# A retention block and a channel mix in one written order: mu's loads on SyncE, block 2 in another form, all pieces in a new order

## The chip, the cores and the metric

The kernel runs on one core of a Trainium2 chip. The metric is the device time of one execution in microseconds (us); lower is better. The core has TensorE (PE, matrix products, with its weight loads shown apart as PEld), VectorE (DVE), ScalarE (ACT), GpSimd (POOL) and SyncE (SP). Here POOL and SP do no arithmetic: they issue transfers (DMAs) between the chip's memory (HBM) and the core's memory (SBUF). PE writes its results to PSUM, eight banks of 512 float32 a partition.

## The reference

Inputs q, k, v have shape (4, 8, 768, 64): batch, heads, time, width. The first stage carries a 64 x 64 state per head through time, and its output, with the heads side by side (512 wide), is the input x of the second stage.

```python
for t in range(S):
    state = gamma[None, :, None, None] * state + np.einsum('bhd,bhe->bhde', k[:, :, t], v[:, :, t])
    y[:, :, t] = scale * np.einsum('bhd,bhde->bhe', q[:, :, t], state)
...
xk = mu_k * x + (1.0 - mu_k) * x_prev
xr = mu_r * x + (1.0 - mu_r) * x_prev
k = np.maximum(xk @ w_k, 0.0)
v = k * k @ w_v
r = 1.0 / (1.0 + np.exp(-(xr @ w_r)))
return (r * v).astype(np.float32)
```

x_prev is x one time step earlier; w_k is 512 x 1024, w_v 1024 x 512, w_r 512 x 512. The output is 4 x 768 x 512 float32.

## The kernel before

Time is cut into blocks of 256 tokens: three to a batch, twelve in all, n = 0 to 11. The step-by-step recurrence is replaced by products within a block (scores of q and k under a causal mask, then times v) and by a state carried between the three blocks of a batch. Blocks 0, 3, 6, 9 begin a batch and need no state; blocks 2, 5, 8, 11 end one and pass none on.

Nothing is scheduled by a compiler. The string ORDER (lines 28 to 79) lists all pieces of work, and the loop at lines 809 to 824 emits them one by one. Each engine executes its own pieces in that order, and waits at a piece whose inputs aren't there, so that what stands behind it on the same engine waits too. A word is code.arguments, with `@` and digits for the PSUM banks and `~` and a letter for the engine (v DVE, a ACT, p POOL, s SP). The first argument is the block n. The codes:

- `lq`, `lk`, `lv` (line 239) load q, k, v of a block. Those on POOL convert q and k to float16 on the way. The first half of block 0's q and k (heads 0 to 3, `lq.0.0.2` and `lk.0.0.2`) comes over SP as float32 into a staging place, and `cq`, `ck` (line 266) convert it on ACT. `mu` (line 739) loads mu_k and mu_r in four small transfers, issued by ACT in before.
- `Tq`, `Tk` (line 294) transpose on PE; `Eq`, `Ek` (lines 320 to 340) copy the result to SBUF on ACT. `tq`, `tk` transpose by DMA, issued by SP, for blocks 9 to 11.
- `vs` (line 276) scales v, on DVE. `S` are the scores (line 378, PE), `M` masks them (line 412, DVE).
- `C` is the block's contribution to the state (line 436, PE), `U` sums it (line 469, mostly DVE), `G` decays it (line 484).
- `I`, `Y`, `J` are the block's output on PE: from the state (`I`, `J`) and from the masked scores times v (`Y`). `I.2` reads the result of `U.2.0`. `D` (line 564, DVE) brings it to SBUF as x, transposed.
- `dx` and `X.n.w.j` (lines 588 and 607, DVE) form xk (w = 0) and xr (w = 1), a quarter j of the width each.
- `K.n.g` (line 627, PE) is a piece of xk @ w_k and needs all four X.n.0.*; `Qa`, `Qb` (ACT) take relu and square. `R` (PE) and `s` (ACT) are the gate, and need X.n.1.*. `V` (PE) is the product with w_v, `O` (DVE) multiplies with the gate, `st` stores over SP. `Vc`, `Oc`, `sc` do the last half block in two column halves.
- `wk`, `wr`, `wv` load the weights over POOL, wk in two halves. `gy` are powers of gamma.
- `z.c` (line 755) multiplies zeros into a bank that nobody reads: c // 4 float32 products and c % 4 float16 ones, 512 columns each, a float32 one counting as four units. They use no data and fill time on PE.

A block has one of three forms, by two lists at lines 17 and 22. Blocks 6 to 11 (HALF) treat a block as four chunks of 64 tokens. Blocks in WIDE (2 to 5 in before) are held with one half of the tokens on the partitions per load: each of k and v comes in two transfers, whose rows are 256 bytes (one token of one head), and the scores are 16 products of 128 weight columns. The remaining ones (0 and 1) hold two neighbouring tokens per partition: one transfer with rows of 512 bytes, and 32 score products of 64 weight columns. Which form a block takes is asked for in `split` (line 235), `scale_v`, `scores`, `masked`, `state` and `intra` (lines 276 to 560).

Of the kernel before, what the change touches and what calls it, by code (L numbers as in the profile page):

```python
# [39 lines left out]
R.1.0@2 R.1.1@3 Qb.1.1 s.1.0 Tq.3@2 s.1.1 Eq.3~a C.3@67 Tk.3@4 Ek.3~a R.0.0@3 s.0.0 Tk.4@2  # L40
S.3.0@01 wv.0~p dx.2~v X.2.0.0 X.2.0.2 X.2.0.1 X.2.0.3 X.2.1.1 S.3.1@45 Ek.4~a K.2.0@3 lq.7~p
Tq.4@2 M.3.1~v U.3.0~a U.3.1 Qa.2.0 wv.1~p Eq.4~a K.2.3@6 Qa.2.3 M.3.0~v K.2.1@7 S.4.1@45
S.4.0@23 vs.4~v M.4.0~v K.2.2@6 Qb.0.2 I.3@01 Y.3 C.4@23 G.3~a M.4.1~v U.4.0 lk.5~p Qb.1.0
Qa.2.2 V.1.0.0@6 lq.5~p I.4@45 Qa.2.1 Qb.2.1 X.2.1.3 J.3 D.3~v Y.4 V.0.1.0@7 V.0.0.0@0 J.4 U.4.1
Tq.7@23 Eq.7~a V.1.1.0@1 V.1.1.1 G.4~a Qb.2.0 dx.3~v V.0.0.1 Tk.5@2 Ek.5~a D.4~v dx.4~v V.0.1.1
Qb.2.3 V.1.0.1 Tq.5@2 X.3.0.3 X.3.0.1 X.3.0.2 Eq.5~a X.3.0.0 K.3.1@3 Qa.3.1 K.3.3@4 O.1.1 O.0.0
S.5.0@01 O.1.0 O.0.1 lv.5~p lq.6~p M.5.0~v S.5.1@23 vs.5~v K.3.2@5 Qa.3.3 lk.6~p Qb.3.3 K.3.5@4
M.5.1~v X.2.1.0 Qa.3.2 X.2.1.2 Tq.6@67 Qa.3.5 Tk.6@01 Eq.6~a lv.6~p lv.7~p Ek.6~a C.5@5 U.5.0
X.3.1.0 Qb.3.1 K.3.0@4 Qa.3.0 lk.7~p K.3.7@6 S.6@23 Qb.3.2 M.6~v I.5@01 Y.5 vs.6~v V.2.1.0@7
R.2.1@2 lv.10~p Qb.2.2 Qa.3.7 K.3.4@6 st.0.0 vs.7~v Qb.3.7 s.2.1 st.0.1 V.2.1.1 Tk.7@45 Qb.3.5  # L50
Qa.3.4 X.3.1.3 X.3.1.1 Qb.3.0 C.6@23 st.1.0 J.5 Ek.7~a X.3.1.2 R.2.0@6 lv.8~p U.6.0~a D.5~v
U.6.1 U.6.2 U.6.3 V.2.0.0@4 s.2.0 K.3.6@6 dx.5~v Qa.3.6 lq.8~p lk.8~p st.1.1 R.4.1@5 I.6@01
O.2.1 st.2.1 X.5.0.1 s.4.1 G.6~a V.2.0.1 O.2.0 X.5.1.0 X.5.0.3 R.3.1@6 s.3.1 C.7@23 U.7.0 S.7@45
Y.6 M.7~v V.3.1.0@7 X.5.0.2 D.6~v R.4.0@6 lk.9~p Qb.3.4 vs.8~v V.3.0.0@4 R.3.0@5 X.5.1.2 s.4.0
Qb.3.6 V.4.1.0@6 V.3.0.1 V.3.1.1 X.5.1.3 V.4.1.1 U.7.1 U.7.2 X.5.1.1 I.7@01 U.7.3 Tk.8@23 O.3.1
s.3.0 O.3.0 R.5.1@7 Ek.8~a st.3.1 lv.9~p dx.6~v X.5.0.0 s.5.1 C.8@45 Tq.8@23 Y.7 K.5.0@7 O.4.1
vs.9~v st.4.1 Eq.8~a D.7~v K.5.3@6 dx.7~v X.6.0.2 G.7~v Qa.5.0 Qb.5.0 st.2.0 lq.10~p tq.10~s
K.5.1@7 Qa.5.1 X.6.0.3 X.6.0.1 Qa.5.3 K.5.2@2 Qa.5.2 st.3.0 lk.10~p tk.10~s lv.11~p U.8.0 U.8.1
U.8.2 R.5.0@7 tk.9~s s.5.0 X.6.0.0 V.4.0.0@6 V.4.0.1 O.4.0 Qb.5.1 lk.11~p lq.9~p Qb.5.3
V.5.0.0@7 V.5.1.0@2 S.8@01 M.8~v I.8@45 X.6.1.3 Qb.5.2 V.5.0.1 K.6.4@6 X.6.1.1 O.5.0 Qa.6.4  # L60
K.6.7@3 Qa.6.7 K.6.3@6 Qa.6.3 X.6.1.0 lq.11~p X.6.1.2 K.6.1@3 Qa.6.1 Y.8 D.8~v C.9@01 Qb.6.1
vs.10~v U.9.0~a S.10@67 M.10~v U.9.1 dx.8~v X.8.0.3 X.8.0.2 Qb.6.3 K.6.6@3 X.8.0.0 Qb.6.7 Qa.6.6
Qb.6.6 V.5.1.1 K.6.2@4 Qa.6.2 X.8.0.1 Qb.6.2 K.6.5@3 tq.9~s Qa.6.5 R.6.1@4 s.6.1 tq.11~s st.5.0
K.6.0@6 O.5.1 U.9.2 U.9.3 G.9~v R.6.0@7 s.6.0 R.7.1@4 Qb.6.4 s.7.1 st.5.1 K.8.3@7 Qa.8.3 S.9@23
tk.11~s I.9@45 Qa.6.0 Qb.6.0 Qb.6.5 C.10@01 U.10.0 M.9~v R.7.0@7 s.7.0 U.10.1 U.10.2 U.10.3
K.8.2@6 K.8.1@2 Qa.8.1 vs.11~v Qb.8.1 V.6.0.0@7 Y.9 I.10@01 C.11@23 G.10~v V.6.0.1 Qa.8.2
V.7.1.0@6 D.9~v K.8.0@4 Qa.8.0 Qb.8.0 Qb.8.2 U.11.0 U.11.1 U.11.2 V.7.1.1 dx.9~v O.7.1 st.7.1
Qb.8.3 I.11@23 Y.10 D.10~v dx.10~v X.9.0.0 S.11@45 M.11~v X.9.0.2 V.7.0.0@6 V.7.0.1 V.6.1.0@0
V.6.1.1 V.8.0.0@1 V.8.0.1 X.9.0.1 V.8.1.0@4 V.8.1.1 st.4.0 X.9.0.3 K.9.0@5 O.7.0 K.9.4@6 X.9.1.1
Qa.9.0 Qa.9.4 Qb.9.4 X.9.1.0 O.6.0 st.6.0 Qb.9.0 X.9.1.3 X.8.1.2 Y.11 X.9.1.2 O.6.1 K.9.2@5  # L70
Qa.9.2 Qb.9.2 K.9.6@6 Qa.9.6 X.8.1.3 K.9.7@7 Qa.9.7 Qb.9.7 K.9.1@0 Qa.9.1 Qb.9.1 K.9.3@5 Qa.9.3
Qb.9.3 R.10.0@7 R.9.1@0 s.9.1 st.6.1 D.11~v R.9.0@5 s.9.0 st.7.0 X.8.1.1 K.9.5@6 V.10.1.0@5
Qa.9.5 Qb.9.5 Qb.9.6 V.10.0.0@6 X.8.1.0 dx.11~v R.8.1@0 s.8.1 V.9.1.0@2 R.8.0@0 X.11.0.2
X.11.1.3 X.11.0.0 X.11.0.3 X.11.0.1 K.11.1@3 s.8.0 K.11.3@0 Qa.11.3 O.8.0 st.8.0 s.10.0
V.9.0.0@1 Qa.11.1 Qb.11.1 K.11.2@0 Qa.11.2 O.8.1 st.8.1 K.11.0@7 X.11.1.2 V.10.0.1 Qb.11.2
# [7 lines left out]
def kernel(  # L83
# [543 lines left out]
    def keys(e, n, g, u=None):  # L627
# [11 lines left out]
        for i in range(w):  # L639
            fo = w * g + i  # L640
            for co in range(NCO):
# [3 lines left out]
                    start=(i == 0 and co == 0), stop=(co == NCO - 1), skip_group_check=True,  # L645
                )

    def relued(e, n, g, *u):
# [2 lines left out]
        nc.scalar.activation(out=kr, in_=banks("K", n, g, *u), func=AF.Relu)  # L651
# [87 lines left out]
    def load_mu(e):  # L739
        for w, x in enumerate((moe_mu_k, moe_mu_r)):  # L740
            y = x.rearrange("(x r c) -> x r c", x=2, c=D)
            for hp in range(2):
                nc.scalar.dma_start(
                    out=mu8[w * NCO : (w + 1) * NCO, low(hp)], in_=y[:, 1:3] if hp else y[:, 0:4:3]
                )

# [108 lines left out]
```

## Time and profile before

| | us |
|---|---|
| median of 3 runs (155.16 to 155.71) | 155.42 |
| the profiled execution | 155.54 |
| its span, first to last instruction | 153.7 |
| PE busy | 147.1 |
| DVE busy | 128.1 |
| ACT busy | 94.4 |
| POOL busy | 62.1 |

A row of the timeline gives start, length, engine, line, operation, output<-input and, in brackets, how long the engine had been idle and what released it. A name with a q behind the engine (SPq, ACTq, POOLq) is a transfer's issue. The chain of work that ended last is followed back from the last instruction; each of its pieces has a start and a length. The engine's busy time counts products of zeros like any other.

### The profile page before, as it was taken

What the parts mean: (1) busy time and instruction counts of PE and PEld (TensorE: products, weight loads), DVE (VectorE), ACT (ScalarE), POOL (GpSimd) and SP (SyncE); (2) the same over time, 40 slices, a digit from 0 to 9 for tenths busy, and PEclk for the clock granted to TensorE, in tenths of its full rate; (3) what the DMA queues carried; (4) which work ended last, traced back from release to release, by engine and by line L of the source; (5) the groups of instructions that cost most, each with busy time, mean ns of one, the idle gap of its engine ahead of it and who ended that gap; (6) DMA issues with size and microseconds to landing.
All of it is one profiled execution on the core that took longest, in us unless ns stands there. A gap on an engine that the chain in (4) does not pass through costs nothing.

```text
span 153.7 us, 4956 instructions
## 1 busy us (share of the span) xinstructions
PE 147.1 (96%) x2129; PEld 82.7 (54%) x2129; DVE 128.1 (83%) x204; ACT 94.4 (61%) x172; POOL 62.1 (40%) x77
## 2 busy tenths in 40 slices
PE   7799899999999999999999999999999999999991
...
DVE  1379999999989999999999996999999999421551
...
GB/s 138 264 234 194 182 237 235 157 196 203 194 188 203 249 226 194 11 236 156 255 178 249 219 156 161 183 62 106 35 4 141 0 70 141 0 0 136 68 205 136
DMA packets 56525, 23.83 MB, mean 155 GB/s; under 512 B 48056, under 2 KB 52024, under 8 KB 56504
## 3 DMA queue, kind: packets, MB, share of 16 engines
...
q10 hardware_dynamic: 456, 0.32, 0.8%
...
HBM read 24.31 MB, written 6.29 MB: 199 GB/s over the span
## 4 chain that ended last, share of the span: by engine, by line
PE 70%; DVE 14%; DMA 6%; ACT 4%; issue 2%; ACTq 2%; DVEq 0%
PE ps L684 24%; PE ps L672 12%; PE ps L632 10%; PE ps L642 9%; DMA kT<-k 6%; DVE a L417 3%; DVE xk L618 3%; DVE dx L592 2%; DVE vs L277 2%; PE ps L504 2%; PE ps L765 2%; DVE xT L577 2%; PE ps L308 2%; PE ps L372 1%; PE ps L303 1%
## 5 line engine op out<-in xcount | busy, mean ns | idle before, releaser
L684 PE MATMUL ps<-wv,k2s 128*128 128x512 f16 x184 | 43.9, 380 | 0.2 <-ACT kr L651 0.2
L651 ACT ACTIVATE kr<-ps 128x512 f32<-128x512 f32 x48 | 27.8, 594 | 23.4 <-PE ps L632 14.9
L684 PEld LDWEIGHTS <-k2s 128*128 128x128 f16 x184 | 17.3, 98 | 19.1
L690 DVE SCALAR_TENSOR_TENSOR os<-ps,rs 128x512 f32<-128x512 f32 x23 | 15.1, 683 | 12.9 <-PE ps L684 6.5
L672 PE MATMUL ps<-wr,xr 128*128 128x512 f16 x96 | 24.0, 380 | 0.0
L642 PE MATMUL ps<-xk,wk 128*128 128x256 f16 x192 | 23.6, 273 | 0.1
L256 POOL DMA_DIRECT2D v<-in_v_dram x20 | 18.0, 917 | 13.8 <-DVE vs L277 10.9
L632 PE MATMUL ps<-xk,wk 128*128 128x512 f16 x96 | 22.8, 380 | 0.0
L417 DVE TENSOR_TENSOR a<-ps,c_sb 128x1024 f16<-128x1024 f32 (+1 forms) x20 | 21.8, 1109 | 0.8 <-PE ps L393 0.8
L678 ACT ACTIVATE rs<-ps 128x512 f32<-128x512 f32 x24 | 14.3, 594 | 11.4 <-PE ps L672 8.8
L642 PEld LDWEIGHTS <-wk 128*128 128x128 f16 x192 | 18.1, 98 | 4.4 <-DVE xk L618 0.5
L618 DVE SCALAR_TENSOR_TENSOR xr<-dx,mu,xT 128x256 f16<-128x256 f32 (+1 forms) x36 | 19.3, 564 | 0.0
L618 DVE SCALAR_TENSOR_TENSOR xk<-dx,mu,xT 128x256 f16<-128x256 f32 (+1 forms) x36 | 18.9, 567 | 0.3
L256 POOL DMA_DIRECT2D k<-in_k_dram x20 | 17.8, 916 | 2.6 <-DMA wv<-in_moe_w_v_dram 1.2
L277 DVE TENSOR_TENSOR vs<-v,csm_sb 128x1024 f16<-128x1024 f32 x12 | 14.5, 1214 | 2.7 <-DMA v<-in_v_dram 2.7
L659 ACT ACTIVATE k2s<-kr 128x512 f16<-128x512 f32 x24 | 14.7, 626 | 0.4
L592 DVE TENSOR_TENSOR dx<-xT 128x1024 f32<-128x1024 f32 x12 | 14.6, 1219 | 0.2
L663 ACT ACTIVATE k2s<-kr 128x512 f16<-128x512 f32 x24 | 14.5, 626 | 0.3
L632 PEld LDWEIGHTS <-wk 128*128 128x128 f16 x96 | 9.0, 98 | 10.5 <-issue 0.2
L672 PEld LDWEIGHTS <-xr 128*128 128x128 f16 x96 | 9.0, 98 | 10.0
L262 ACT COPY qT<-ps 128x1024 f16<-128x1024 f16 (+1 forms) x10 | 9.2, 925 | 7.5 <-PE ps L314 3.4
L262 ACT COPY kT<-ps 128x1024 f16<-128x1024 f16 (+1 forms) x10 | 9.3, 934 | 7.1 <-PE ps L303 3.4
...
## 6 DMA issues: line engine op xcount, KB each, us to landing
out_dram<-os SPq DMA_DIRECT2D x23, 256.0 KB, 3.9
v<-in_v_dram POOLq DMA_DIRECT2D x20, 256.0 KB, 6.3
k<-in_k_dram POOLq DMA_DIRECT2D x21, 128.0 KB, 7.1
q<-in_q_dram POOLq DMA_DIRECT2D x13, 128.0 KB, 7.4
q<-in_q_dram POOLq DMA_DIRECT2D x5, 256.0 KB, 8.1
...
wk<-in_moe_w_k_dram POOLq DMA_DIRECT2D x2, 256.0 KB, 9.6
```

Source lines behind the costliest of these rows:

```text
L256: e.dma_start(out=to[:, i, hs], in_=src[:, i])
L262: e.copy(out=out, in_=in_)
L277: e.tensor_tensor(out=VS(n), in0=V32(n).rearrange("p (h i d) -> p i h d", i=2, h=H), in1=gks[:, int(half(n) or wide(n)), :, :, None].to_br ...
L417: nc.vector.tensor_tensor(out=dst, in0=dst if n in SPLITM else src, in1=mask[:, None, None, :].to_broadcast(list(dst.shape)), op=ALU.mult,)
L592: e.tensor_tensor(out=DX(k)[:, :, m * TM + t0 : m * TM + t1], in0=x[:, :, c + t0 : c + t1], in1=x[:, :, c - 1 + t0 : c - 1 + t1], op=ALU.s ...
L618: nc.vector.scalar_tensor_tensor(out=XM[w](k)[:, j, t0:t1], in0=DX(k)[:, j, t0:t1], scalar=mu[:, w * NCO + j : w * NCO + j + 1], in1=x[:, ...
L632: nc.tensor.matmul(banks("K", n, g), lhsT=wk16[:, co, g * P : g * P + P], rhs=XM[0](k)[:, co, :], start=(co == 0), stop=(co == NCO - 1),)
L642: nc.tensor.matmul(pz[:, i, :], lhsT=wk16[:, co, fo * P : fo * P + P], rhs=XM[0](k)[:, co, m * TM + t0 : m * TM + t1], start=(i == 0 and c ...
L651: nc.scalar.activation(out=kr, in_=banks("K", n, g, *u), func=AF.Relu)
L672: nc.tensor.matmul(banks("R", n, tb), lhsT=XM[1](k)[:, co, t : t + P], rhs=wr16[:, co, :], start=(co == 0), stop=(co == NCO - 1),)
L684: nc.tensor.matmul(banks("V", n, tb), lhsT=K2(n)[:, fo, tb * P : tb * P + P], rhs=wv16[:, fo, :], start=(fo == 0), stop=(fo == NFO - 1),)
L690: nc.vector.scalar_tensor_tensor(out=OS(2 * n + tb), in0=banks("V", n, tb), scalar=1.0 / (KSC * KSC), in1=RS(2 * n + tb), op0=ALU.mult, op ...
```

## The change

mu's four loads go to the engine that the word names, and the new order names SP (`mu~s`), between the staged k and the staged q. Block 2 leaves WIDE, so it is loaded and multiplied as blocks 0 and 1 are. The first words of zeros become `z.9` for `z.8`; over the whole order there are 40 units of zeros for 32. All pieces are written in a new order, 622 words for 624; the products of the two stages are the same but for block 2's form. A function `keys_by_row` with the code `Kp` is added, and no word of the order calls it.

```diff
-WIDE = (2, 3, 4, 5)
+WIDE = (3, 4, 5)
...
+KP = ()
...
-gy.0 lq.0.0.2~s mu lk.0.0.2~s cq.0.0.2~a lv.0~p z.8@7 Tq.0.0.2@0 ck.0.0.2~a vs.0~v Eq.0.0.2~a
-z.3@1 Tk.0.0.2@1 Ek.0.0.2~a z.3@2 S.0.0.0.2@23 lk.0.2.4~p S.0.1.0.2@45 M.0.1.0.2~v Tk.0.2.4@1
-gy.1~a Ek.0.2.4~a lq.0.2.4~p C.0@67 Tq.0.2.4@0 Eq.0.2.4~a U.0.0~v lv.1~p lk.1~p M.0.0.0.2~v
-U.0.1 z.3@4 S.0.1.2.4@45 M.0.1.2.4~v I.0@01 mt@2 me lq.1~p S.0.0.2.4@67 M.0.0.2.4~v lq.2~p G.0~a
-vs.1~v z.4@3 Y.0 Tk.1@6 Ek.1~a D.0~v dx.0~v z.3@3 Tq.1@7 X.0.0.0 Eq.1~a X.0.1.1 wk.1~p C.1@23
-U.1.0 lk.2~p z.4@4 S.1.1@45 M.1.1~v z.1@0 I.1@01 wk.0~p S.1.0@67 M.1.0~v X.0.0.3 Tq.2@4 Eq.2~a
-z.2@5 Y.1 lv.2~p X.0.0.1 X.0.0.2 z.1@5 K.0.2@4 Tk.2@5 D.1~v X.0.1.0 dx.1~v Qa.0.2 X.0.1.2
-X.1.0.0 Ek.2~a K.0.3@0 Qa.0.3 Qb.0.3 X.1.0.2 X.1.0.1 S.2.1@67 K.0.0@5 Qa.0.0 K.0.1@0 X.1.0.3
-K.1.2@1 K.1.0@5 Qb.0.0 wr~p X.1.1.0 Qa.0.1 U.1.1 G.1~a vs.2~v X.0.1.3 Qa.1.0 Qa.1.2 Qb.0.1
-X.1.1.1 C.2@0 U.2.0 K.1.1@3 Qa.1.1 I.2@45 lv.3~p M.2.1~v S.2.0@01 K.1.3@2 lq.3~p Qb.1.2 R.0.1@3
...
+lk.0.0.2~s ck.0.0.2~a lv.0~p lk.0.2.4~p gy.0 z.9@7 Tk.0.0.2@0 Ek.0.0.2~a vs.0~v mu~s lq.0.2.4~p
+lq.0.0.2~s cq.0.0.2~a z.5@1 Tq.0.0.2@1 Eq.0.0.2~a z.3@2 S.0.1.0.2@23 S.0.0.0.2@45 M.0.0.0.2~v
+Tk.0.2.4@1 gy.1~a Ek.0.2.4~a C.0@67 Tq.0.2.4@0 Eq.0.2.4~a z.3@4 S.0.1.2.4@45 M.0.1.0.2~v lv.1~p
+U.0.0~v I.0@23 U.0.1 M.0.1.2.4~v lq.1~p lk.1~p lk.2~p S.0.0.2.4@01 M.0.0.2.4~v z.4@6 Y.0 vs.1~v
+Tq.1@0 mt@1 me lv.2~p D.0~v dx.0~v z.2@6 C.1@67 G.0~a Tk.1@1 Eq.1~a X.0.0.3 X.0.0.2 z.4@4 Tk.2@0
+Ek.1~a X.0.0.1 U.1.0 X.0.0.0 U.1.1 G.1~a Ek.2~a z.2@4 I.1@45 wk.0~p S.1.0@23 M.1.0~v S.1.1@67
+M.1.1~v z.8@1 Y.1 vs.2~v K.0.1@6 Qa.0.1 lq.2~p Tq.2@7 Eq.2~a wk.1~p C.2@0 lq.3~p K.0.0@1 Qa.0.0
+Qb.0.0 D.1~v dx.1~v U.2.0 I.2@23 X.1.0.1 X.1.0.3 S.2.1@45 S.2.0@67 lk.3~p X.0.1.3 X.1.0.0
+X.1.0.2 K.0.2@0 Qa.0.2 K.0.3@1 Qa.0.3 Qb.0.3 M.2.0~v Qb.0.1 X.0.1.0 Qb.0.2 M.2.1~v wr~p K.1.1@0
+Qa.1.1 K.1.2@1 Qa.1.2 K.1.0@6 Qa.1.0 Tk.3@4 Qb.1.0 Y.2 X.1.1.0 Ek.3~a Tq.3@1 K.1.3@0 lq.4~p
...
+Qa.8.1 lv.11~p O.5.0 s.7.0 st.5.0 K.8.2@2 Qa.8.2 I.9@67 Qb.6.6 U.9.3 tq.11~s st.5.1 G.9~v
+C.10@01 U.10.0 U.10.1 S.9@45 M.9~v K.8.3@3 vs.11~v Qa.8.3 Qb.8.0 V.7.0.0@2 V.7.0.1 U.10.2 U.10.3
+Qb.8.1 R.7.1@3 s.7.1 Y.9 I.10@45 C.11@01 O.7.0 Qb.8.3 st.4.0 V.6.1.0@3 V.6.1.1 D.9~v dx.9~v
+G.10~a U.11.0 U.11.1 U.11.2 tk.11~s O.6.1 V.7.1.0@6 V.6.0.0@7 V.6.0.1 O.6.0 st.6.0 Qb.8.2
+S.11@01 M.11~v I.11@23 Y.10 D.10~v V.7.1.1 dx.10~v X.9.0.3 X.9.0.0 V.8.1.0@7 st.7.0 X.9.0.1
...
-                nc.scalar.dma_start(
+                (e or nc.scalar).dma_start(
                     out=mu8[w * NCO : (w + 1) * NCO, low(hp)], in_=y[:, 1:3] if hp else y[:, 0:4:3]
...
+    def keys_by_row(e, n, gp, co):
```

In the new order POOL's loads stand as v.0, the second halves of k.0 and q.0, v.1, q.1, k.1, k.2, v.2, wk.0 (three transfers), q.2, wk.1 (three); in before as v.0, the second halves of k.0 and q.0, v.1, k.1, q.1, q.2, wk.1 (three), k.2 (two), wk.0 (three), v.2 (two).

More of the change, by code (lines that the diff above doesn't have):

```diff
@@ L34 @@
-U.1.0 lk.2~p z.4@4 S.1.1@45 M.1.1~v z.1@0 I.1@01 wk.0~p S.1.0@67 M.1.0~v X.0.0.3 Tq.2@4 Eq.2~a
-z.2@5 Y.1 lv.2~p X.0.0.1 X.0.0.2 z.1@5 K.0.2@4 Tk.2@5 D.1~v X.0.1.0 dx.1~v Qa.0.2 X.0.1.2
-X.1.0.0 Ek.2~a K.0.3@0 Qa.0.3 Qb.0.3 X.1.0.2 X.1.0.1 S.2.1@67 K.0.0@5 Qa.0.0 K.0.1@0 X.1.0.3
-K.1.2@1 K.1.0@5 Qb.0.0 wr~p X.1.1.0 Qa.0.1 U.1.1 G.1~a vs.2~v X.0.1.3 Qa.1.0 Qa.1.2 Qb.0.1
-X.1.1.1 C.2@0 U.2.0 K.1.1@3 Qa.1.1 I.2@45 lv.3~p M.2.1~v S.2.0@01 K.1.3@2 lq.3~p Qb.1.2 R.0.1@3
-Qa.1.3 lk.3~p M.2.0~v X.1.1.2 Y.2 lk.4~p lq.4~p Qb.1.3 s.0.1 lv.4~p X.1.1.3 vs.3~v J.2 D.2~v
@@ L40 @@
[L40 to L75, printed above, removed]
@@ L76 @@
-Qb.11.3 V.9.1.1 Qa.11.0 R.10.1@0 Qb.11.0 V.10.1.1 O.9.1 st.9.1 s.10.1 X.11.1.0 X.11.1.1 V.9.0.1
-R.11.1@0 V.11.0.0@7 R.11.0@4 O.9.0 st.9.0 V.11.0.1 O.10.1 s.11.1 st.10.1 s.11.0 O.10.0 st.10.0
-O.11.0 st.11.0 Vc.11.1.0@4 Oc.11.1.0 sc.11.1.0~s Vc.11.1.1@6 Oc.11.1.1 sc.11.1.1~a
+lk.0.0.2~s ck.0.0.2~a lv.0~p lk.0.2.4~p gy.0 z.9@7 Tk.0.0.2@0 Ek.0.0.2~a vs.0~v mu~s lq.0.2.4~p
+lq.0.0.2~s cq.0.0.2~a z.5@1 Tq.0.0.2@1 Eq.0.0.2~a z.3@2 S.0.1.0.2@23 S.0.0.0.2@45 M.0.0.0.2~v
+Tk.0.2.4@1 gy.1~a Ek.0.2.4~a C.0@67 Tq.0.2.4@0 Eq.0.2.4~a z.3@4 S.0.1.2.4@45 M.0.1.0.2~v lv.1~p
@@ new lines @@
+Qa.1.1 K.1.2@1 Qa.1.2 K.1.0@6 Qa.1.0 Tk.3@4 Qb.1.0 Y.2 X.1.1.0 Ek.3~a Tq.3@1 K.1.3@0 lq.4~p
+X.1.1.1 X.0.1.1 X.0.1.2 R.0.0@6 X.1.1.3 lk.4~p lv.3~p Eq.3~a D.2~v dx.2~v R.0.1@7 s.0.0 s.0.1
+X.1.1.2 Qa.1.3 S.3.1@23 X.2.0.0 Qb.1.1 S.3.0@45 X.2.0.2 R.1.1@6 s.1.1 Tq.4@0 Eq.4~a R.1.0@7
+X.2.0.3 lv.4~p s.1.0 Tk.4@6 Ek.4~a M.3.0~v X.2.0.1 K.2.2@4 K.2.3@5 Qa.2.3 Qa.2.2 M.3.1~v
+S.4.1@01 Qb.2.3 S.4.0@23 X.2.1.2 vs.3~v C.3@67 X.2.1.1 M.4.1~v wv.0~p lq.7~p U.3.0~a K.2.1@5
+vs.4~v K.2.0@4 U.3.1 I.3@01 Y.3 C.4@67 Qa.2.1 Qb.2.1 M.4.0~v G.3~a U.4.0 Qb.1.2 wv.1~p U.4.1
@@ new lines @@
+V.0.1.0@5 V.1.1.0@2 I.4@67 Qa.2.0 Qb.2.0 J.3 Y.4 X.2.1.0 Qb.1.3 G.4~a V.1.0.0@4 Qb.2.2 D.3~v
+dx.3~v Tq.7@01 J.4 Eq.7~a D.4~v V.0.0.0@3 V.0.0.1 lq.6~p dx.4~v X.3.0.0 lk.6~p V.1.0.1 V.0.1.1
+lk.5~p O.1.0 V.1.1.1 Tq.6@01 Eq.6~a X.2.1.3 Tk.6@67 X.3.0.1 V.2.1.0@4 Ek.6~a V.2.1.1 X.3.0.2
+X.3.0.3 Tk.5@0 Ek.5~a lq.5~p Tq.5@6 X.3.1.1 K.3.0@7 Qa.3.0 K.3.5@0 lv.5~p Qa.3.5 Eq.5~a O.0.0
+lk.7~p X.3.1.2 O.1.1 K.3.1@7 Qa.3.1 O.0.1 Qb.3.1 K.3.3@5 Qa.3.3 st.0.1 vs.5~v S.5.0@23 X.3.1.3
+M.5.0~v lv.6~p S.5.1@01 C.5@7 U.5.0 M.5.1~v R.2.1@6 K.3.4@5 s.2.1 Qa.3.4 Qb.3.4 K.3.7@6 Qa.3.7
@@ new lines @@
+I.5@23 S.6@01 vs.6~v M.6~v lq.8~p lv.7~p O.2.1 Y.5 K.3.6@5 Qb.3.0 st.0.0 Qa.3.6 X.3.1.0 Qb.3.6
+C.6@67 Tk.7@01 Ek.7~a U.6.0~a Qb.3.3 J.5 D.5~v lv.8~p dx.5~v R.2.0@4 K.3.2@5 s.2.0 R.3.0@2
+Qa.3.2 Qb.3.2 s.3.0 Qb.3.7 lk.10~p U.6.1 U.6.2 U.6.3 V.2.0.0@3 V.2.0.1 vs.7~v O.2.0 lk.8~p
+I.6@01 lv.9~p X.5.0.2 X.5.0.1 S.7@45 M.7~v Tq.8@67 st.2.0 X.5.0.0 R.3.1@2 Qb.3.5 Eq.8~a
+V.3.1.0@3 R.4.1@6 V.3.1.1 G.6~a s.3.1 X.5.0.3 st.1.1 vs.8~v st.2.1 s.4.1 C.7@45 lk.11~p U.7.0
+U.7.1 Y.6 D.6~v X.5.1.2 K.5.1@2 Qa.5.1 K.5.0@6 Qa.5.0 X.5.1.0 K.5.3@2 Qa.5.3 Qb.5.3 lq.11~p
@@ new lines @@
+V.4.1.0@6 V.4.1.1 U.7.2 I.7@01 U.7.3 Tk.8@45 O.3.1 G.7~a Ek.8~a C.8@23 X.5.1.1 R.4.0@7 s.4.0
+O.4.1 K.5.2@6 U.8.0 X.5.1.3 U.8.1 U.8.2 Qb.5.0 S.8@45 st.1.0 Y.7 Qa.5.2 I.8@23 dx.6~v R.5.1@7
+Qb.5.2 Qb.5.1 lq.10~p R.5.0@6 s.5.1 D.7~v V.4.0.0@7 V.4.0.1 st.3.1 M.8~v dx.7~v X.6.0.1 X.6.0.3
+lk.9~p vs.9~v X.6.1.0 st.4.1 V.3.0.0@4 V.3.0.1 V.5.0.0@5 V.5.1.0@0 V.5.0.1 V.5.1.1 X.6.0.2
+X.6.0.0 K.6.3@1 O.3.0 s.5.0 tk.10~s tq.10~s K.6.7@4 Qa.6.3 Qa.6.7 Qb.6.7 st.3.0 X.6.1.2 O.4.0
+S.10@67 O.5.1 M.10~v Y.8 C.9@01 U.9.0~a tk.9~s K.6.1@4 lv.10~p X.6.1.3 K.6.2@6 D.8~v K.6.5@7
```

27 lines of the change are left out of this document (26 added, 1 removed).

## The prediction

> **What bounds the kernel now.** I read the page first, for the shares of the engines and the chain.
>
> ```profile
> span 153.7 us, 4956 instructions
> PE 147.1 (96%) x2129; PEld 82.7 (54%) x2129; DVE 128.1 (83%) x204; ACT 94.4 (61%) x172; POOL 62.1 (40%) x77
> PE   7799899999999999999999999999999999999991
> DVE  1379999999989999999999996999999999421551
> PE 70%; DVE 14%; DMA 6%; ACT 4%; issue 2%; ACTq 2%; DVEq 0%
> ```
>
> TensorE (PE) is full from the seventh slice on and holds 70% of the chain that ended last; VectorE (DVE) is almost as full up to slice 34. So the end is set by three things: when PE begins to have all the real work that it can do, how much work is then left, and how long it waits after that. The busy share doesn't tell the first, since products of zeros count as busy. The chain in order of time does; columns are start, length, what.
>
> ```profile
> 4.94 0.63 ACT q L262
> ...
> 5.61 0.64 PE ps L314 x8
> 6.25 1.39 PE ps L765 x3
> 7.64 0.57 PE ps L314 x7
> 8.21 1.39 PE ps L765 x3
> 9.60 0.35 PE ps L393 x16
> ...
> 11.69 0.41 DVE t L482
> 12.10 1.25 DVE a L417 x2
> ...
> 14.40 1.23 DVE xT L577
> ...
> 15.64 1.24 DVE dx L592
> ...
> 19.25 1.21 DVE a L417
> ...
> 24.82 1.66 DVE xk L618 x4
> ...
> 27.21 1.15 DVE vs L277
> ...
> 28.40 0.32 PE ps L447 x8
> ...
> 31.24 0.86 PE ps L672 x4
> ...
> 37.42 0.55 PE ps L385 x16
> ...
> 82.14 3.60 PE ps L642 x32
> ```
>
> Up to 9.60 us a line of ScalarE (ACT) casts, transpositions and zeros leads to the first scores; from there to 28.40 VectorE is the line; then PE takes over with C.2. One more reading: three products of zeros take 1.39 us at 8.21, 0.46 us each, while four of the same 512 columns take 0.86 at 31.24, 0.22 each. Up to about 9.60 PE runs at half its later rate.
>
> How long PE waits after it took over is in the waits from 28 us on (columns: engine, line, what it waited for: us, times, longest).
>
> ```profile
> PEld L642 <- DVE xk L618: 0.5, 1, 0.5
> PEld L372 <- DMA kT<-k: 0.5, 1, 0.5
> PE ps L684 <- ACT kr L651: 0.2, 1, 0.2
> ```
>
> These make about 1.1 us in 125. PE loses almost nothing behind the head, so what matters is how much real work PE still owes at the moment when it takes over.
>
> **The change part by part.** The new head casts k first and has the four loads of mu on SyncE (SP) between k's and q's. The rows for their price are the timeline's, and the time from issue to landing.
>
> ```profile
> 0.74 0.45 SPq L245 DMA_DIRECT2D k2s<-in_q_dram  x1
> 1.05 3.78 PE L758 MATMUL ps<-zero 128*128 128x512 f32 x4 [1.05 <-DVE xT L737]
> 2.98 0.62 ACTq L743 DMA_DIRECT2D mu<-in_moe_mu_k_dram  x1
> 5.47 0.61 ACT L262 CAST k<-k2s 128x512 f16<-128x512 f32 x1
> 6.29 0.59 ACT L262 COPY qT<-ps 128x512 f16<-128x512 f16 x1 [0.21 <-PE ps L314]
> 7.94 1.23 DVE L277 TENSOR_TENSOR vs<-v,csm_sb 128x1024 f16<-128x1024 f32 x1 [2.69 <-DMA v<-in_v_dram]
> 10.00 0.69 DVE L417 TENSOR_TENSOR a<-ps,c_sb 128x512 f16<-128x512 f32 x1 [0.84 <-PE ps L393]
> 150.14 0.33 SPq L717 DMA_DIRECT2D out_dram<-os  x1
> k2s<-in_q_dram SPq DMA_DIRECT2D x1, 256.0 KB, 3.3
> k2s<-in_k_dram SPq DMA_DIRECT2D x1, 256.0 KB, 4.0
> q<-in_q_dram POOLq DMA_DIRECT2D x13, 128.0 KB, 7.4
> ```
>
> *k's side.* k is issued at 0.74 and lands 3.3 to 4.0 later, at 4.0 to 4.7. ACT no longer issues mu, which kept it until 4.94, so the cast is done near 5.3. PE has nine units of zeros instead of eight (3.78 / 8 = 0.47 each, the f32 products counting four), from 1.05 to 5.3. Tk of the first half then runs from 5.3 to 5.9. The extra product of zeros costs nothing; k's cast hides it.
>
> *q's side.* No row shows a load of mu on SP, so I take ACT's: 0.62, 0.65 with its gap. k's issue ends at 1.2, four of mu make 2.6, and q is issued at 3.8 instead of 0.74. I take the 4.0 of the later of the two staged loads: landing at 7.8, cast to 8.45 (0.61), Tq to 9.1 (0.64), copy to 9.8 (0.59 and the hand-over). The bounds of the landing are 3.3 and, if it has to share with GpSimd's (POOL's) loads, their 7.4. In between PE does five units of zeros, 5.9 to 8.3 at 0.47, and behind Tq three more: 9.1 to 10.0 if the rate doubles at 9.60 as before. So the first scores start at 10.0, and since the first mask is now of the group of scores that comes second, it waits for 0.35 more: 10.0 + 0.35 + 0.40 (9.60 to 10.00 before) = 10.75, against 10.00.
>
> *VectorE from there to the takeover.* In the new order PE meets I.2 behind two groups of K of block 0, and I.2 reads U.2.0. Before it stand on DVE: four half masks 2.5, U six less one = five at 0.41 = 2.05, vs.1 and vs.2 2.3, D.0 and D.1 2.46, dx.0 and dx.1 2.4, the four xk pieces of block 0 1.66, M.1 2.42: 15.8 us. The same count for before, from its first mask to the end of vs.2, gives 18.7 where the chain has 28.36 - 10.00 = 18.4; so I take 15.5. U.2.0 ends at 26.25 and I.2 starts at 26.3. Up to there PE has slack: the last filler, eight units of zeros ahead of Y.1 (8 x 0.22 = 1.7 us), ends before M.1 does, and the other fillers stand in front of waits too; all 40 units instead of 32 cost nothing as long as these covers stand.
>
> *What PE owes.* At 28.40 before had done six groups of K, S.2.1 and no C.2. At 26.3 after has done two groups of K and C.2. Owed more: four groups, 3.60 (the row at 82.14), and S.2.1, less C.2's 0.32. Block 2 in block 0's form has 32 products of scores in two lots of 0.35 (L393 x16) for two of 0.28 (0.55 at 37.42), so 0.15 more; its intra products and its state cost the same within 0.1. Together 3.7 us for a start 2.1 us earlier: PE is **1.6 us behind**.
>
> *Behind the takeover.* I made running sums of the DVE and the PE pieces in the written order from 26.3 on. Nowhere in the new order does a K, R, Y, C or I come up on PE more than 0.5 us ahead of the VectorE piece that it needs. Of the 1.1 us of waits above I let 0.4 go; the bounds are all of them (-1.1) and as much again (+1.1).
>
> *Loads.* Block 2's k and v as one load each of 512-byte rows save two issues of POOL, which nothing waits for: DVE's and PE's waits behind 10 us name no load of k or v. I cost them at nothing; the risk is in their place in the queue, below.
>
> Sum: +1.6 - 0.4 = +1.2 us. The profiled execution took 155.54 us around its span of 153.7, the runs' median is 155.42; the same tail stands behind both orders, so 155.42 + 1.2 = **156.6 us**.
>
> **The rivals.**
>
> *The rate doubles earlier.* In before PE stood still from 4.83 to 5.61 (zeros to Tq); in after Tk follows the zeros and zeros follow Tk, so PE is busy from 1.05 to 8.3 without a gap. If that brings the doubling to about 8, Tq takes 0.35 and the three units 0.65: scores start at 9.5, 0.5 us earlier, and the time is 156.1. For it: all of the slow products stand in the first 9.6 us. Against it: 3.78 us of zeros in one piece didn't do it. The Trainium skill, "TensorE: Matmul & The Clock Gate", Part 1, has the half rate end after a busy window of about 3.4 us that runs free; by that rule 7 us without a gap hold a whole window, and this rival would be the case.
>
> *Faster: SP issues mu for little.* SP's cheapest issue (0.33, at 150.14) could make the four of mu 1.3 us instead of 2.6, and with 3.3 to landing q is there at 5.9. Then Tq waits only for the five zeros; that alone gives nothing while they run at 0.47. Together with the earlier rate they end at 7.2, the scores start at 8.4, and the masks start with the end of vs.0, at 9.2: 1.55 us earlier. PE is then level with before at the takeover and wins 0.4 to 1.1 of the later waits: 154.7. It decides at Tq: it has to start by 7.3.
>
> *Loads late.* POOL's queue seems to keep eight loads going: in before each issue that waits does so for the eighth before it.
>
> ```profile
> 16.87 0.59 POOL L725 DMA_DIRECT2D wk<-in_moe_w_k_dram  x1 [2.38 <-DMA q<-in_q_dram]
> ...
> 21.91 0.93 POOL L256 DMA_DIRECT2D v<-in_v_dram  x1 [0.55 <-DMA wk<-in_moe_w_k_dram]
> 23.29 0.89 POOL L256 DMA_DIRECT2D v<-in_v_dram  x1 [0.45 <-DMA wk<-in_moe_w_k_dram]
> 87.35 8.93 DMA kT<-k
> ```
>
> q.2 landed at 16.87 as the seventh load; now it is the twelfth, behind v.2 and half of wk. From 16.87 to 23.29 three to four such amounts landed, about 1.9 us each, so I put wk's first half at 21.5 (needed at 23.5) and q.2 at 23.4 (needed at 24.4): a margin of 1 us. If it fails by 1 us, or q's landing takes the 7.4, or the last DMA transposition on SP (tk.11, now behind three stores and tq.11; one took 8.93) holds S.11, PE loses 1 to 3 us: 158.5.
>
> *The later waits vanish.* If the new order leaves none of the 1.1 us, 156.6 becomes 155.9.
>
> **How the numbers follow.** Forecast 156.6 (156.0 to 157.3): 0.45. Earlier rate, 156.1: 0.18. Loads late, 158.5: 0.15. Faster, 154.7: 0.12. No later waits, 155.9: 0.10. A measurement of this kernel tells about 0.3% (0.47 us) from no change. Slower than 155.9: 0.9 of the forecast, two thirds of the earlier rate, all late loads, half of the last, 0.71 together; faster than 154.95: most of the faster case, 0.12; 0.17 between. The range: 155.0, which leaves out most of the faster case, to 158.2, which leaves out the worse half of the late loads.
>
> **What would show it.** Right: mu's four issues on SP at 0.6 us each, q's cast at 7.8 to 8.5, the first mask at 10.7, I.2 on PE at 26.3 released by U.2.0, two K groups before it, and few waits of PE behind it. Wrong: the first mask before 10 or behind 11.5; Tq.2 or K released by a DMA; products of zeros at 0.22 before 8 us; PE waits behind 30 us of over 1.5 us in sum.

## The result

The changed kernel takes 170.22 us (median of 4 runs, 168.01 to 174.01) for 155.37 us of the kernel before on the same chip: 1.086 times as long (95% interval 1.077 to 1.095). The ratio leaves two disturbed runs out, so by it the time is 168.7 us. The direction was forecast, the size was not: 156.6 us, with a range up to 158.2. The profiled execution took 169.54 us.

The page of the profile after, the same rows as those shown of before:

```profile
span 167.7 us, 5031 instructions
PE 149.8 (89%) x2171; PEld 85.1 (51%) x2171; DVE 127.8 (76%) x202; ACT 95.0 (57%) x180; POOL 60.3 (36%) x75
PE   7719999999999999999999960399999999999992
DVE  2404899999998999999999970299699999920442
PEclk9965999999999999999999996569999999999998
PE 53%; DMA 18%; issue 12%; POOL 6%; DVE 4%; ACT 3%; SPq 2%; DVEq 0%; POOLq 0%
```

PE's row has two holes that before hasn't, at slice 3 (8 to 13 us) and at slices 24 to 26 (96 to 109 us). The row PEclk is the clock that was granted to PE, in tenths of full speed; in these places and just behind them it falls to 0.5 and 0.6. Everything between is as full as in before. Two places, then, hold the 14.0 us of span.

The timeline of after up to the first mask (start, length, engine, line, what, and in brackets the idle time ahead and its releaser):

```profile
1.26 1.50 SPq L757 DMA_DIRECT2D mu<-in_moe_mu_k_dram  x2
2.80 1.27 SPq L757 DMA_DIRECT2D mu<-in_moe_mu_r_dram  x2
...
3.86 0.62 ACT L263 CAST k<-k2s 128x512 f16<-128x512 f32 x1 [0.73 <-DMA k2s<-in_k_dram]
...
4.11 0.40 SPq L246 DMA_DIRECT2D k2s<-in_q_dram  x1
...
5.20 0.64 PE L315 MATMUL ps<-c_sb,k 128*64 128x128 f16 x8
...
11.31 0.62 ACT L263 CAST q<-k2s 128x512 f16<-128x512 f32 x1 [4.85 <-DMA k2s<-in_q_dram]
11.98 0.64 PE L315 MATMUL ps<-c_sb,q 128*64 128x128 f16 x8 [4.75 <-ACT q L263]
...
12.56 1.46 PE L779 MATMUL ps<-zero 128*128 128x512 f16 x3
...
14.64 1.29 DVE L418 TENSOR_TENSOR a<-ps,c_sb 128x512 f16<-128x512 f32 x2 [6.04 <-PE ps L394]
```

The staged q is issued at 4.11, 0.3 us later than forecast, but lands at 11.3: 7.2 us after its issue, not 4.0. PE stands for 4.75 us. The first mask is at 14.64 where it was forecast at 10.75 and stood at 10.00 in before.

The second hole, first by rows of POOL's queue and of PE in after, then by its windows (length, then busy time and instructions of PE, PEld, DVE, ACT and POOL, the granted clock, the share of the transfer engines and GB/s):

```profile
70.72 3.51 POOL L257 DMA_DIRECT2D k<-in_k_dram  x4 [13.37 <-PE ps L430]
...
80.29 1.77 POOL L257 DMA_DIRECT2D k<-in_k_dram  x2 [4.27 <-PE ps L430]
82.03 3.53 POOL L257 DMA_DIRECT2D q<-in_q_dram  x4
...
90.74 1.90 POOL L257 DMA_DIRECT2D v<-in_v_dram  x2
...
107.39 0.64 PE L373 MATMUL ps<-qT,kT 64*64 64x64 f16 x32 [8.21 <-DMA qT<-q]
```

```profile
102.00:108.00 6.00, 0.61 (x46) 0.65 (x50) 0.00 (x0) 0.00 (x0) 0.00 (x0) 0.50 1.51 189
108.00:114.00 6.00, 6.00 (x100) 2.98 (x90) 5.61 (x8) 2.02 (x5) 0.00 (x0) 0.68 0.14 29
```

POOL's queue stands 13.37 us in front of the load of block 10's k. k has four places in SBUF (RING, line 25), so that load writes where block 6's k lies, and the last reader there is C.6 (L430). Behind it wait the loads of k.8, v.9, k.11, q.11, q.10 and the rest, and 4.27 us more are lost in front of k.11, for C.7. So fourteen transfers, the rows from 80.29 to 90.74, are issued in one go, q.10 among them. The chain of work that ended last goes from the landing of q.10 through its DMA transposition to PE:

```profile
30.34 0.43 DVE tg L483
...
30.81 0.31 PE ps L505 x8
...
84.64 5.99 DMA q<-in_q_dram
...
90.77 16.48 DMA qT<-q
...
109.10 5.81 PE ps L633 x20
```

The transposition takes 16.48 us, and PE stands for 8.2 of them. Then 20 products take 5.81 us, 0.29 each, where such a product takes 0.22 at full rate: 1.4 us more; and the 1.7 us of small products ahead of them ran in the low clock as well, some 0.9 us more. By this count, an estimate, the hole costs about 10.5 us. (The first two rows are the release of I.2 and I.2 itself, used below.)

### The profile page after: what moved, and what is told of

The parts are those of the page before. It is cut to its first block, busy times and chain, and to the rows that moved or that the text cites. A ratio compares the mean times of both kernels' runs of the same rounds, so it can differ in the third digit from the quotient of the medians.

```text
span 167.7 us, 5031 instructions
## 1 busy us (share of the span) xinstructions
PE 149.8 (89%) x2171; PEld 85.1 (51%) x2171; DVE 127.8 (76%) x202; ACT 95.0 (57%) x180; POOL 60.3 (36%) x75
## 4 chain that ended last, share of the span: by engine, by line
PE 53%; DMA 18%; issue 12%; POOL 6%; DVE 4%; ACT 3%; SPq 2%; DVEq 0%; POOLq 0%
PE ps L698 13%; PE ps L643 10%; DMA qT<-q 10%; PE ps L686 8%; PE ps L633 8%; DMA k2s<-in_q_dram 4%; DMA q<-in_q_dram 4%; POOL k L257 3%; POOL v L257 2%; SPq L757 2%; DVE xT L578 1%; PE ps L505 1%; PE ps L315 1%; PE ps L779 1%; PE ps L772 1%
## 5 line engine op out<-in xcount | busy, mean ns | idle before, releaser
L698 PE MATMUL ps<-wv,k2s 128*128 128x512 f16 x184 | 42.4, 379 | 0.0
L633 PE MATMUL ps<-xk,wk 128*128 128x512 f16 x96 | 23.6, 396 | 0.0
L643 PE MATMUL ps<-xk,wk 128*128 128x256 f16 x192 | 23.1, 273 | 0.0
L257 POOL DMA_DIRECT2D k<-in_k_dram x18 | 15.9, 901 | 17.9 <-PE ps L430 17.6
L643 PEld LDWEIGHTS <-wk 128*128 128x128 f16 x192 | 18.2, 98 | 3.4
L257 POOL DMA_DIRECT2D v<-in_v_dram x18 | 16.3, 922 | 2.1 <-DVE xr L619 0.8
L633 PEld LDWEIGHTS <-wk 128*128 128x128 f16 x96 | 9.5, 102 | 11.9 <-issue 2.0
L257 POOL DMA_DIRECT2D q<-in_q_dram x12 | 10.8, 926 | 1.5 <-DMA v<-in_v_dram 1.0
```

Source lines behind the costliest of these rows:

```text
L257: e.dma_start(out=to[:, i, hs], in_=src[:, i])
L633: nc.tensor.matmul(banks("K", n, g), lhsT=wk16[:, co, g * P : g * P + P], rhs=XM[0](k)[:, co, :], start=(co == 0), stop=(co == NCO - 1),)
L643: nc.tensor.matmul(pz[:, i, :], lhsT=wk16[:, co, fo * P : fo * P + P], rhs=XM[0](k)[:, co, m * TM + t0 : m * TM + t1], start=(i == 0 and c ...
L698: nc.tensor.matmul(banks("V", n, tb), lhsT=K2(n)[:, fo, tb * P : tb * P + P], rhs=wv16[:, fo, :], start=(fo == 0), stop=(fo == NFO - 1),)
```

## The experiments

Theory: the loss has two parts that don't depend on each other. The staged q lands late, and POOL's order issues block 10's and the later loads too late and in a crowd. Rivals: the second wait takes over what the first gives back; only q.10's own place counts, not the crowd; mu's small transfers hold q on SP's queue; the half rate of PE or block 2's form is what costs. Lines of kernels made from after are after's, of those made from before are before's. A ratio is to before on the same chip, with its 95% interval.

**One: mu issued by ACT again, nothing else** (a_mu_act).

```diff
-lk.0.0.2~s ck.0.0.2~a lv.0~p lk.0.2.4~p gy.0 z.9@7 Tk.0.0.2@0 Ek.0.0.2~a vs.0~v mu~s lq.0.2.4~p
+lk.0.0.2~s ck.0.0.2~a lv.0~p lk.0.2.4~p gy.0 z.9@7 Tk.0.0.2@0 Ek.0.0.2~a vs.0~v mu lq.0.2.4~p
```

> The changed kernel with one word changed: mu is issued by ScalarE again, so that SyncE issues the staged q right behind the staged k. Two independent waits (my theory): q lands near 5.3 us instead of 11.3, the first mask starts at 10.2 to 11.0 instead of 14.6, TensorE keeps its full rate, and all that follows comes 3.8 to 4.6 us earlier, TensorE's wait for the transposed q of block 10 included: 165 to 166.5 us. Rival, the second wait swallows the first: block 10's q comes when the transfers let it, whatever the head does; the wait at the scores of block 10 grows by what the head wins, and the time stays within 1.5 us of the changed kernel's 169.5.

166.75 us, ratio 1.074 (1.068 to 1.080), between what the theory and the rival gave. The first mask is at 10.95, 3.7 us earlier, and the time 1.2% of before less, about 1.9 us (the intervals just overlap). PE's wait for the transposition grew from 8.2 to 9.2 us: part of the head's gain is swallowed there. The head alone doesn't explain the result.

**Two: POOL's order alone** (b_pool). Only words of loads move; POOL's words from the load of block 10's k on, in their order:

```diff
-lk.10~p lk.8~p lv.9~p lk.11~p lq.11~p lq.10~p lk.9~p lv.10~p lq.9~p lv.11~p
+lk.8~p lv.9~p lq.10~p lk.10~p lk.9~p lq.9~p lv.10~p lk.11~p lq.11~p lv.11~p
```

> The changed kernel with nothing but the order of GpSimd's late loads changed: the loads of block 8's k, block 9's v and block 10's q stand ahead of block 10's k, which has to wait for C.6, and those of block 9's k and q and block 10's v ahead of block 11's k, which has to wait for C.7. My theory: TensorE's 8.2 us wait at block 10's scores comes from GpSimd standing 13.4 us at one load whose buffer was still in use, with block 10's q behind it. Then that wait falls under 1.5 us, the slow rate behind it goes too, and the time is 159.5 to 161.5 us. Rival, the DMA transposition itself is slow (16.5 us) because the queues are crowded at that time: it stays over 12 us, TensorE still waits over 4 us, and the time is over 165 us.

159.62 us, ratio 1.030 (1.026 to 1.034), as expected. No row of PE's waits names a transposition any more. The rows of the transfers, with the median time from issue to landing last, of after and then of this run:

```profile
k2s<-in_q_dram SPq DMA_DIRECT2D x1, 256.0 KB, 7.2
...
qT<-q SPq DMA_TRANSPOSE x3, 16.5
```

```profile
k2s<-in_q_dram SPq DMA_DIRECT2D x1, 256.0 KB, 6.8
...
qT<-q SPq DMA_TRANSPOSE x3, 5.8
```

The order of ten words of loads is worth 5.6% of before's time here, 8.7 us; q's late landing stays.

**Three: both** (c_both).

> Both edits: mu issued by ScalarE, and GpSimd's late loads in the other order. My theory: the two waits are all that went wrong with the forecast, so the time is the forecast's sum with q early, 155.5 to 157.3 us. Rival, the new order of the pieces or block 2's form costs time by itself: over 158 us.

156.21 us (12 runs, 155.00 to 157.87), ratio 1.007 (1.003 to 1.012), as expected. The two parts together are about the whole of the loss. The first mask is at 12.43 here, 1.5 us later than in experiment one, though ACT issues mu between its copy of k and its cast of q in both (here from 5.88 to 9.06). PE's rows behind its gap for q differ; here:

```profile
9.77 0.64 PE L315 MATMUL ps<-c_sb,q 128*64 128x128 f16 x8 [2.50 <-ACT q L263]
10.34 1.46 PE L779 MATMUL ps<-zero 128*128 128x512 f16 x3
```

In experiment one the same transpositions start at 9.38 and take 0.41, and the three products of zeros take 0.82. So 0.4 us of the 1.5 is the later start, and the other 1.1 us is PE's half rate behind a gap of 2.50 us, where a gap of 2.68 us in experiment one left the full rate.

**Four: mu on SP, but behind both staged loads** (d_q_first).

```diff
-lk.0.0.2~s ck.0.0.2~a lv.0~p lk.0.2.4~p gy.0 z.9@7 Tk.0.0.2@0 Ek.0.0.2~a vs.0~v mu~s lq.0.2.4~p
-lq.0.0.2~s cq.0.0.2~a z.5@1 Tq.0.0.2@1 Eq.0.0.2~a z.3@2 S.0.1.0.2@23 S.0.0.0.2@45 M.0.0.0.2~v
+lk.0.0.2~s ck.0.0.2~a lv.0~p lk.0.2.4~p gy.0 z.9@7 Tk.0.0.2@0 Ek.0.0.2~a vs.0~v lq.0.2.4~p
+lq.0.0.2~s mu~s cq.0.0.2~a z.5@1 Tq.0.0.2@1 Eq.0.0.2~a z.3@2 S.0.1.0.2@23 S.0.0.0.2@45 M.0.0.0.2~v
```

> The changed kernel with mu still issued by SyncE, but behind both staged loads instead of between them. My theory: it is q's place behind mu's four issues that cost the head, not which engine issues mu; the time equals that of the kernel with mu on ScalarE within 0.7 us, 165 to 166.5 us. Rival, SyncE's issuing mu delays q's landing or mu itself (mu is needed by the first pieces of xk): 1.5 us or more above the kernel with mu on ScalarE.

164.18 us, ratio 1.058 (1.051 to 1.065). That is 2.6 us less than with ACT issuing mu, where I had expected the same. The timeline and PE's waits:

```profile
1.25 0.49 SPq L246 DMA_DIRECT2D k2s<-in_q_dram  x1
...
6.36 0.62 ACT L263 CAST q<-k2s 128x512 f16<-128x512 f32 x1
...
9.15 1.29 DVE L418 TENSOR_TENSOR a<-ps,c_sb 128x512 f16<-128x512 f32 x2
```

```profile
PE ps L373 <- DMA qT<-q: 8.8, 1, 8.8
```

Issued at 1.25, q has landed long before ACT casts it, and the first mask is at 9.15, 0.85 us ahead of before's. What the first experiment missed are ACT's own mu issues in front of the cast. The wait for the transposition stays, at 8.8 us.

**Five: this and POOL's order together** (i_q_pool).

> The changed kernel with two orders mended: mu on SyncE behind both staged loads, and GpSimd's late loads in the other order. In the kernel with mu back on ScalarE the q cast stood behind mu's four issues there (first mask 12.4 us); with mu behind q on SyncE the first mask came at 9.2. My theory: VectorE's line from the first mask to I.2 and TensorE behind it carry the 3.2 us through, so the time is 152.3 to 153.7 us, faster than the kernel before (154.9 on this chip) by about 1%. Rival, TensorE's debt binds later: an earlier head only makes it wait at masks and xk pieces that VectorE delivers no earlier; 154.5 to 156.2.

153.29 us (6 runs, 152.75 to 153.51) for 154.38 of before: ratio 0.990 (0.985 to 0.995). This version beats both kernels. Its rows of the same kind, the transfers and one window:

```profile
k2s<-in_q_dram SPq DMA_DIRECT2D x1, 256.0 KB, 3.9
...
qT<-q SPq DMA_TRANSPOSE x3, 5.0
```

```profile
30.00:148.00 118.00, 118.00 (x1717) 66.45 (x1715) 103.42 (x157) 77.80 (x147) 37.66 (x43) 1.00 0.94 146
```

PE is busy in all of the 118 us behind 30. The first mask and I.2 of this run:

```profile
9.21 1.29 DVE L418 TENSOR_TENSOR a<-ps,c_sb 128x512 f16<-128x512 f32 x2 [0.19 <-PE ps L394]
...
24.72 0.31 PE L505 MATMUL ps<-qT,tg 64*64 64x128 f16 x8 [0.21 <-DVE tg L483]
```

Against experiment four only POOL's order differs: 6.8% of before, 10.6 us, which is what the hole of after came to above. Against experiment two only mu's place on SP's queue differs: 4.0%, 6.2 us, for a first mask at 9.21 in place of 14.27.

**Six: only q.10's load moved, ahead of k.10's** (e_lq10).

```diff
-lk.10~p lk.8~p lv.9~p lk.11~p lq.11~p lq.10~p lk.9~p lv.10~p lq.9~p lv.11~p
+lq.10~p lk.10~p lk.8~p lv.9~p lk.11~p lq.11~p lk.9~p lv.10~p lq.9~p lv.11~p
```

> The changed kernel with one load moved: block 10's q ahead of block 10's k on GpSimd; the other late loads still stand behind C.6 and C.7. If the late load of q alone made the wait, the transposition is issued at about 88 us behind k's, lands within 9 us, TensorE waits under 1.5 us and the time is 160 to 162 us. If the crowd of late loads between 80 and 107 us makes the transposition slow, as I now think more likely, it is issued at 88 but still takes 12 us or more, TensorE waits 3 to 7 us and the time is 164 to 168 us.

168.82 us (2 runs), ratio 1.091 (1.083 to 1.100): nothing won. Queue rows (two of POOL, one of SP) and the chain's row of this run:

```profile
71.00 3.51 POOL L257 DMA_DIRECT2D k<-in_k_dram  x4 [10.90 <-PE ps L505]
...
80.27 1.77 POOL L257 DMA_DIRECT2D k<-in_k_dram  x2 [3.99 <-PE ps L430]
...
88.77 2.67 SPq L349 DMA_TRANSPOSE qT<-q  x1
```

```profile
88.77 17.73 DMA qT<-q
```

q.10 is now loaded early. POOL still stands at k.10 and k.11, and its later loads still come in a bunch up to 90.9. The transposition stands in SP's queue until 88.77, behind another one, and takes 17.73 us. So the crowd counts and not q.10's own load; the time fell outside what I had expected even for that case, since the transposition was no quicker for starting 2 us earlier.

**Seven: more zeros over q's wait** (f_zeros), on the kernel of experiment two: `z.17@1` for `z.5@1`.

> The kernel with the mended order of GpSimd's loads (159.6 us; mu still ahead of q on SyncE) with 17 units of zeros instead of 5 between the transpositions of k and q, which fill TensorE's wait of 4.6 us for q. If that wait costs more than its length because TensorE's rate falls to half in it, the products behind it run at full rate now, the first mask comes 1.0 to 1.4 us earlier (14.3 to about 13.1) and the time is 158.2 to 158.7 us. Rival, the rate doesn't matter here, since VectorE's and ScalarE's steps set the pace: first mask within 0.3 us of 14.3 and time within 0.4 us of 159.6.

159.7 us, ratio 1.033 (1.027 to 1.038), no better than without. The PE rows of the timeline, two on each side of the gap:

```profile
5.76 3.70 PE L772 MATMUL ps<-zero 128*128 128x512 f32 x8
9.30 0.38 PE L779 MATMUL ps<-zero 128*128 128x512 f16 x1
12.50 0.63 PE L315 MATMUL ps<-c_sb,q 128*64 128x128 f16 x8 [2.82 <-ACT q L263]
13.06 1.46 PE L779 MATMUL ps<-zero 128*128 128x512 f16 x3
```

Sixteen units of zeros take 3.70 us, 0.23 each, so PE had its full rate from 5.76 on and the zeros ended at 9.7. A gap of 2.82 us was left, and behind it products took 0.49 again. In this execution q landed 7.7 us after its issue and the first mask is at 15.15, 0.9 us later than in experiment two. The zeros didn't reach q's cast, so this run doesn't measure the price of the half rate; experiments one and three do, 1.1 us of first mask.

**Eight: mu's move alone, in before** (g_before_mu): SP issues mu between its staged q and its staged k.

```diff
-gy.0 lq.0.0.2~s mu lk.0.0.2~s cq.0.0.2~a lv.0~p z.8@7 Tq.0.0.2@0 ck.0.0.2~a vs.0~v Eq.0.0.2~a
+gy.0 lq.0.0.2~s mu~s lk.0.0.2~s cq.0.0.2~a lv.0~p z.8@7 Tq.0.0.2@0 ck.0.0.2~a vs.0~v Eq.0.0.2~a
...
-                nc.scalar.dma_start(
+                (e or nc.scalar).dma_start(
```

> Kernel before with mu's four loads alone moved: SyncE issues them, between the staged q and the staged k. Theory (what stands behind mu on SyncE's queue is issued some 2.9 us later and lands after POOL's first loads, 7 us instead of 4): the staged k is issued at 4 us instead of 1.2, is cast at 11 to 11.5 instead of 5.3, the first mask stands at 14 to 15 instead of 10.0, and the time is 3 to 5 us over the kernel before of the same chip. Rival (only the issue moves, the landing stays 4 us): k cast at 8.3, first mask at 12, time 1 to 2 us over.

161.18 us, ratio 1.037 (1.030 to 1.043): 5.7 us more, somewhat over what I expected. Timeline:

```profile
4.07 0.40 SPq L245 DMA_DIRECT2D k2s<-in_k_dram  x1
...
11.99 0.62 ACT L262 CAST k<-k2s 128x512 f16<-128x512 f32 x1 [7.44 <-DMA k2s<-in_k_dram]
...
15.32 0.69 DVE L417 TENSOR_TENSOR a<-ps,c_sb 128x512 f16<-128x512 f32 x1 [6.22 <-PE ps L393]
```

With before's order and before's block 2 the same edit does the same: what is staged behind mu is issued at 4.07, lands about 7.9 us later, and the first mask is 5.3 us late. The edit alone is dear in both orders.

**Nine: the staged q on ACT's queue** (k_q_act), on the kernel of experiment two. mu stays on SP, and ACT issues q behind its cast of k: `lq.0.0.2~a` behind `ck.0.0.2~a`, in place of `lq.0.0.2~s`.

> As the run with only POOL's order mended (159.62 us, q cast at 10.94), but the staged q is issued by ScalarE behind its cast of k, at about 4.4 us; mu's four loads stay on SyncE. Theory (a load issued behind POOL's first six lands late, since they share the transfer engines): it lands 6.8 to 7.2 us after its issue on any queue, the cast stands at 11.2 to 11.8, the first mask at 14.5 to 15.1, and the time is 1.03 to 1.04 times before's. Rival (mu's small transfers ahead of it on SyncE's own queue hold it): on ScalarE's queue it lands 3.3 to 4.8 us after its issue, the cast stands at 7.7 to 9.2, the first mask at 11 to 12.5, and the time is 1.00 to 1.01 times before's.

159.44 us, ratio 1.028 (1.024 to 1.033).

```profile
3.95 0.41 ACTq L246 DMA_DIRECT2D k2s<-in_q_dram  x1
...
11.43 0.62 ACT L263 CAST q<-k2s 128x512 f16<-128x512 f32 x1 [4.97 <-DMA k2s<-in_q_dram]
```

On another queue, with nothing of mu ahead of it there, q issued at 3.95 lands 7.5 us later. So its place behind mu on SP's queue doesn't hold it. What is left is that POOL's first loads are under way by then; no run took those away, so their part is argued and not shown. (The Trainium skill, "DMA: Bandwidth & Descriptors", section "Issuing engines are not separate DMA queues", says that transfers of all issuing engines run on the same 16 transfer engines and interleave; this run agrees, 7.5 us on ACT's queue for 6.8 on SP's.)

**Ten: block 2's form alone, in before** (h_block2): `WIDE = (3, 4, 5)`, and J.2 left out of the order, since that form doesn't need it.

> The kernel before with block 2 in block 0's form and nothing else changed (block 2's k and v in one load each with 512-byte rows, 32 score products for 16; its state is added in Y, so the piece J.2 goes). My theory: 0.15 us more of products, loads that nothing waits for: within 0.5 us of the kernel before. Rival, the rows of 512 bytes let all loads of the head land earlier and win 0.5 us or more, or the form costs VectorE or TensorE 0.5 us or more.

156.91 us, ratio 1.011 (1.005 to 1.017), where I expected no difference. **Eleven: the reverse** (j_wide2), the version of experiment five with `WIDE = (2, 3, 4, 5)` and J.2 behind Y.2.

> The fastest kernel so far (mu behind both staged loads, block 10's q ahead of its k on POOL, 153.29 us) with block 2 back in its old form: WIDE is 2 to 5 again, J.2 stands behind Y.2. Theory (the form is worth little, and the 1.2 us that the kernel before lost with the new form come from a hole on TensorE at 83 us, 2.1 us for which no semaphore is shown, which only some executions have): 153.3, within 0.7. Rival (the new form itself costs 1.2 to 2.5 us): 150.8 to 152.1. Other side (the old form's four loads of 256-byte rows and 16 more products of weights come back): 154 or more.

156.44 us (12 runs, 155.82 to 158.11), ratio 1.013 (1.009 to 1.017), 2.3% more than experiment five, and in the range that I had given for "other side". Both lost, though they change the form in opposite directions. A row of PE's waits of the tenth, one of its windows, and a row of PE's waits of the eleventh:

```profile
PE ps L642 <- issue: 2.1, 1, 2.1
```

```profile
84.00:96.00 12.00, 10.89 (x101) 6.35 (x101) 8.79 (x14) 4.95 (x9) 0.56 (x1) 0.86 1.71 171
```

```profile
PE ps L505 <- issue: 2.7, 2, 1.5
```

In the profiled executions PE stands for 2.1 and 2.7 us for which no semaphore is shown, at 83 us in the tenth, and at 64.5 and 83.5 us in the eleventh; in the tenth the clock falls to 0.86 behind it. Up to 82 us the tenth's chain is before's within 0.2 us. None of the other profiles has such a row. The holes are 2.7 of the eleventh's 2.8 us of span over experiment five. That speaks for a form that is worth little by itself, but it isn't shown: there is one profile of each, the tenth's is of an execution of 158.22 us, well above its median, and whether the change of form brings the holes with it was not tested. What makes them stays open too: they lie where the transfer engines are full, but before and experiment five are full there too.

## Why the prediction was wrong

- **"I take the 4.0 of the later of the two staged loads"**: this step failed. 7.2 us were measured, and 7.5 and 7.9 where I tried the same elsewhere (experiments nine and eight). The 4.0 came from a load that had been issued at 1.2 us, with POOL's first; at 4.1 four loads of POOL are under way and more follow, and the row of POOL's q said 7.4. The rival "loads late" named that number and then priced it at 1 to 3 us. Its price was 3.9 us at the first mask (14.64 for 10.75). At the end, 5.1 to 5.5 us of first mask are worth 4.4 to 6.2 us (after against experiment four, two against five).
- **"I made running sums of the DVE and the PE pieces"** and, of the loads, **"I cost them at nothing"**: this step failed, and it was the larger one. The sums behind the takeover left out POOL's queue and the DMA transpositions, and the waits that it went by were the old order's. Late loads were looked for at the front of the order and at tk.11, and the prediction never asked which buffer each load of POOL's new queue has to wait for. k.10 in front of k.8 meant a wait for C.6; everything behind it came late and in a crowd, the transposition of q.10 took 16.48 us and PE stood. By pairs of runs that differ in it alone: 8.7 us (after against two), 10.3 (one against three), 10.6 (four against five). The rival suspected the last transposition on SP, tk.11; it was tq.10.
- **The issue of mu on SP** was right: 2.77 us for four, forecast 2.6, so the rival "SP issues mu for little" fell. On k's side Tk came at 5.20, forecast 5.3, but partly by luck: k landed 3.1 us after its issue and its cast was done at 4.48, so the nine units of zeros set Tk's start and k's cast didn't hide the ninth. With q so late that cost nothing.
- **VectorE's 15.5 us from the first mask to U.2.0** held. In after it is 16.1, in experiment five 15.5, from 9.21 to I.2's start at 24.72.
- **"1.6 us behind"** was nearly right, as seen without the two failures. In experiment five I.2 is 1.6 us earlier than forecast, so PE should be level with before, and 0.4 better by the later waits; it is 1.6 us better. Of the 1.1 us of waits behind the takeover all went, not 0.4; the other half us isn't explained.
- **The rival "the rate doubles earlier"** came true and was worth nothing in after: four units of zeros from 5.76 take 1.25 us there, so PE's rate went up before 7. Then PE stood 4.75 us for q, and the next products ran at 0.49 (1.46 us for three).
- **Block 2's form at nothing** is neither shown nor refuted: the change of form cost 1.1% in one direction (experiment ten) and 2.3% in the other (eleven), with the holes in both.

Sum: 156.6, plus 3.9 for the first mask, plus 8.7 to 10.6 for POOL's order, is 169.2 to 171.1; the profiled execution took 169.54, the ratio gives 168.7. The sum is a rough one, since the second wait swallows part of what the first one costs (experiment one). The prediction's chances of a slower kernel add up to 0.72 and not to 0.71, which changes nothing.
